# A triangular solve put on GpSimd, with halved and doubled tiles, fewer rows loaded and a new order

## The chip, the cores and the metric

The kernel runs on one core of a Trainium2 chip. The metric is the device time of one launch in microseconds (us), median of several runs. TensorE is called PE here, its weight loads PEld, VectorE is DVE, ScalarE is ACT, GpSimd is POOL, and SP is SyncE, the queue that issues every DMA of this kernel.

## The reference: a recurrent attention and two feed-forward layers

```python
def _attn_ref(r, k, v, w, a, b):            # each (4, 8, 768, 40)
    state = np.zeros((B, H, D, D))
    for t in range(S):
        y[:, :, t] = np.einsum('bhd,bhde->bhe', rt, state)
        Sa = np.einsum('bhde,bhe->bhd', state, at)
        state_decay = state * wt[:, :, None, :] - np.einsum('bhd,bhe->bhde', Sa, bt)
        state = state_decay + np.einsum('bhd,bhe->bhde', vt, kt)
    return y
...
    x = attn_out.transpose(0, 2, 1, 3).reshape(B * S, H * D)     # (3072, 320)
    h = x @ w_in;  g = h * (1.0 / (1.0 + np.exp(-h)));  x = g @ w_out     # layer 1, d_ff 2048
    h = x @ w_in2; g = np.maximum(0.01 * h, h);         out = g @ w_out2  # layer 2, d_ff 2048
```

The feed-forward weights arrive as float64; the kernel takes their words apart into floats ("decode").

## The kernel before, in words

**Attention in chunks.** The 768 steps are cut into 12 chunks of 64 steps. A chunk is two halves (two batches each), numbered x = 2c and x = 2c+1, so x runs from 0 to 23. Inside a chunk the recurrence is a triangular system per head, which is solved in two diagonal blocks of 32 by 32. Per x there are two functions, and per chunk a third:

- `pre(x)` (line 673) loads the decay products P and their reciprocals Q (tiles pt, qt), the rows of a, b and k, and builds on PE and DVE the triangular matrices (tiles sa, s2). The diagonal blocks go to DRAM (`s2d<-s`). The ring `sa` has four tiles, so `pre(x)` may start writing once the first products of `chain(x-4)` have read theirs; two GpSimd memsets (`sa<-`, 64x512) and a multiplication by P do that.
- `solve(c)` (line 724) loads both halves' blocks from DRAM, spread over the partitions, into `il_mm` ("ilm", one tile), and a start matrix into `il_y` ("ily", one tile) from a DRAM copy `il0d`. Then it does 31 elimination steps of two instructions each, a product into `il_t` ("ilt") and an addition into `il_y`, all `V.tensor_tensor`, thus DVE. The two alternate and each needs the one before. The inverse goes out in 8 DMAs (`yd<-ily`).
- `chain(x)` (line 748) loads the inverse (`yt<-yd`) and all other rows, and does the recurrent part: products of sa with the state (`bank<-tv,sa`), two products with the inverse (`bank<-carved,yt`), the state for x+2, and the output tile `xt`.

**Prefix products.** `prefix(g)` (line 624) makes the cumulative products of w for chunks 4g to 4g+3 in the tile `scratch`, and writes them, plain and transposed, to DRAM (`pd`, `ptd`), then their reciprocals (`qd`, `qtd`). Transposing is `transposed` (line 644): an ACT copy of 8 columns into a spare piece ("room") of `scratch`, then one DMA; 5 of these per matrix. For g = 1, 2 there is one room, so each copy waits for the DMA of the one before. `scratch` also serves the decoding of both layers' weights, in turn.

**Layers.** `moe_block` (line 489) does 256 tokens: transposes of two `xt` tiles, 16 pieces of the hidden dimension (products `bank<-xs,ih`, `il`, `i`; an activation on ACT; a remainder on DVE, `gs<-bank,gs`), and products `bank<-oh,gs`, `ol,gs`. Layer 1's block c needs chunk c's two x. Blocks of layer 1 fill PE between the steps of the attention. Layer 2 begins when the attention's tiles are released, and has 12 blocks of its own.

**What sets the order.** No operation is issued where it is written: `plan.record` (line 161) makes a task of it, and `Plan.run` (line 242) simulates the engines with estimated costs and issues, engine by engine, the task that can start first, and among several the one with the earliest due time. The due times come from the table `DUE` (line 339): per kind of work an offset for the first indices, one for the others, and a spread. `VG` tasks may go to DVE or POOL (`choose`, line 356). The order on each engine is thus fixed before the launch, and every engine works through its own list in order: an instruction that waits holds back all that stand behind it. All instructions recorded this way carry the line of `emit`, L370, so the trace is read by tile names.

Of the kernel before, what the change touches and what calls it, by code (L numbers as in the profile page):

```python
# [12 lines left out]
F32 = mybir.dt.float32  # L13
# [4 lines left out]
ALU = mybir.AluOpType  # L18
# [5 lines left out]
C = 64  # L24
# [34 lines left out]
class Plan:  # L59
# [172 lines left out]
    def hop(self, u, i, t, raw):  # L232
        e = u.engs[i]
        if e == "sync":
            return self.QUEUE + u.lat + self.LAND
        if t.engs == u.engs and not raw:
            return 0.0
        if e == "vector" and t.engs != u.engs:
            return 175.0
        return self.HOP[e]  # L240

    def run(self):
# [97 lines left out]
        "first": ((), -100.0, 0.0),  # L340
        "w1": ((-5.92, -26.13), 35.21, 2.15),
        "load": ((-1.55, -13.17, -4.18, -4.78, -3.25), -0.16, 1.0),
        "pre": ((-4.66, -13.38, -8.98, -1.31, -7.1), -7.87, 6.76),
        "solve": ((-3.08, -4.86, -4.85, -5.45, -11.98), -5.53, 4.21),
        "v": ((), 0.55, 0),
        "rows": ((), 5.99, 0),
        "chain": ((-0.56, -3.13, -3.14, 0.42, -3.28), 0.71, 0),
        "moe": ((0.74, 0.86, -0.46), -0.49, 4.78),
        "prefix": ((26.47, -11.65, 22.35), 25.65, 14.34),
        "w2": ((), 9.32, 10.91),  # L350
        "w2load": ((), 0.0, 0.2),
# [81 lines left out]
def attention_moe_kernel(  # L433
# [11 lines left out]
    x2d = dram.tile([NC, 2, 128, DM], F32, name="x2d")  # L445
    il0d = dram.tile([128, 8, 32], F32, name="il0d")
    w2d = dram.tile([128, 3 * DFF + NF * DM], F32, name="w2d")
# [9 lines left out]
    xo = [const.tile([128, DM], F32, name="xo")] * 2  # L457
    xt = Ring(const.tile([128, DM], F32, name=f"xt{i}") for i in range(4))
    gs = [const.tile([128, 2, TB], F32R, name=f"gs{i}") for i in range(3)]
# [29 lines left out]
    def moe_block(W, layer, get_x, put, gs, xs, xo, turn):  # L489
# [6 lines left out]
        for i in range(2):  # L496
            x = get_x(i)
            ps = plan.bank("h" if layer == 1 else "t", [128, 3, 128], False)
            with plan.group():
                for kt in range(2):  # L500
                    T.transpose(ps[:, kt, :], x[:, kt * 128 : kt * 128 + 128], ident)
                T.transpose(ps[0:64, 2, :], x[:, 256:DM], ident)
            h, l = xs[:, at[i], 0], xs[:, at[i], 1]
            A.copy(h[:, 0:2, :], ps[:, 0:2, :])
            A.copy(h[0:64, 2, :], ps[0:64, 2, :])
            A.copy(h[64:128, 2, :], ps[0:64, 2, :])
            V.tensor_tensor(out=l[:, 0:2, :], in0=ps[:, 0:2, :], in1=h[:, 0:2, :], op=ALU.subtract)
            V.tensor_tensor(out=l[0:64, 2, :], in0=ps[0:64, 2, :], in1=h[0:64, 2, :], op=ALU.subtract)
# [42 lines left out]
    with ExitStack() as c1:  # L551
# [5 lines left out]
        def one(shape, name):  # L557
            return ap.tile(shape, F32, name=name)
# [20 lines left out]
        uvts = many(1, [128, 2, 4, 2, 64], "uvt")  # L579
        zts = Ring(carved[:, 1, 1280 + 320 * i : 1600 + 320 * i].rearrange("p (v e) -> p v e", v=8) for i in range(2))  # L580
        s2s = one([128, 4, 16, 32], "s2")
        s2m = Ring(s2s[0:32, i] for i in range(4))
        s2rs = Ring(s2s[64:128, i, 0:8] for i in range(4))
        yt = many(2, [128, 8, 32], "yt")
        il_mm = one([128, 2, 32, 32], "ilm")
        il_y = one([128, 2, 8, 32], "ily")
        il_t = one([128, 2 * 76], "ilt")
        mask = one([128, 64], "mask")
        scratch = one([128, (C + 1) * (E + 8)], "scratch")

# [24 lines left out]

        il_0 = il_y[:, 0]
        G.memset(il_0, 0.0)
        for base, fill in ((0, -1.0), (32, 0.0)):
            G.affine_select(
                out=il_0, in_=il_0, pattern=[[-128, 8], [32, 32]], compare_op=ALU.is_gt, fill=fill, base=base, channel_multiplier=-1  # L620
            )
        SY.dma_start(out=il0d, in_=il_0)

        def prefix(g):
# [14 lines left out]

            room = il_mm.rearrange("p x i t -> p (x i t)") if g == 0 else wt  # L640
            n = 8 * (C + 1)
            rooms = itertools.cycle([room[:, n * i : n * i + n] for i in range(room.shape[1] // n)])

            def transposed(dst, x):
                for q in range(5):
                    z, qs = next(rooms)[:, : 8 * x.shape[2]].rearrange("p (e t) -> p e t", e=8), slice(8 * q, 8 * q + 8)
                    A.copy(z, x[:, qs])
                    SY.dma_start(
                        out=dst[4 * g : 4 * g + 4, :, qs].rearrange("c x e t -> (c x) (e t)"), in_=z.rearrange("p e t -> p (e t)")
                    )  # L650
# [97 lines left out]
        def chain(x):  # L748
# [19 lines left out]
            SY.dma_start(out=uvt[:, :, :, 1].rearrange("p b u t -> p (b u) t"), in_=xvt[x])  # L768
# [124 lines left out]
        for t in uv:  # L893
            VG.memset(t[0:64], 0.0)
        for t in tp + tt + rbd + uus:
            VG.memset(t, 0.0)
# [265 lines left out]
```

## Time and profile before

| | us |
|---|---|
| median of 3 runs | 1388.38 (1386.92 to 1392.41) |
| profiled execution | 1384.11, of which span 1382.1 |
| PE busy, DVE busy, ACT busy, POOL busy | 1094.7, 904.8, 690.6, 128.6 |
| mean granted TensorE clock | 0.911 |

How to read it: the span goes from the first to the last instruction. Layer 2 alone runs in the last 28% of it, attention and layer 1 together in the rest. Since each engine works in order, an engine's idle time is put down to what its next instruction was waiting for. Idle time counts only where that engine sets the end.

### The profile page before, as it was taken

The page shows a single profiled execution, that of the slowest core. Times are in us where ns is not written, and L with a number is a line of the kernel's source. Part 1 is how long each engine was busy: PE and PEld are TensorE (multiplying, and loading weights), DVE is VectorE, ACT ScalarE, POOL GpSimd, SP SyncE. Part 2 cuts the span into 40 slices and gives each one's busy share as a digit, 9 for nine tenths or more (in the row PEclk, how much of TensorE's full clock was granted, in tenths as well). Part 3 has the DMA queues.
Part 4 walks back from the last instruction along what each step waited for, and adds up shares of the span by engine and source line. Part 5 has one row for each costly group of instructions (what it writes and reads, how often), then busy time and mean ns, then how long its engine had stood idle before and what let it go on. Part 6 is the DMA issues. An engine that isn't in the chain of part 4 may idle for free.

```text
span 1382.1 us, 31698 instructions
## 1 busy us (share of the span) xinstructions
PE 1094.7 (79%) x12370; PEld 1034.3 (75%) x12370; DVE 904.8 (65%) x2211; ACT 690.6 (50%) x1760; POOL 128.6 (9%) x153
## 2 busy tenths in 40 slices
PE   1052077778888697888897879799899999999997
PEld 0041067667777596787787879789899999999997
DVE  8988688494758684858686759584555544445543
ACT  5444373444536364445454536465654444444443
POOL 3430014010310100002010000000000000000000
PEclk9985569798989899899999899899999999999999
DMA  9874347665858487575766766564511010000000
GB/s 220 200 185 139 97 121 167 128 173 115 186 133 186 120 192 164 138 178 133 172 165 149 163 157 157 144 135 106 164 55 28 20 30 20 20 20 25 16 11 22
DMA packets 356838, 164.09 MB, mean 119 GB/s; under 512 B 304712, under 2 KB 323272, under 8 KB 356296
## 3 DMA queue, kind: packets, MB, share of 16 engines
q1 hardware_dynamic: 356680, 161.99, 48.8%
q8 instruction: 99, 1.62, 0.5%
q14 instruction: 59, 0.48, 0.1%
HBM read 126.09 MB, written 35.84 MB: 117 GB/s over the span
## 4 chain that ended last, share of the span: by engine, by line
PE 46%; DMA 22%; DVE 19%; SPq 5%; ACT 4%; issue 4%; POOL 0%; DVEq 0%; ACTq 0%
PE bank L370 46%; DMA ilm<-s2d 6%; DVE scratch L370 5%; SPq L370 5%; DMA yd<-ily 3%; DVE ilt L370 3%; DVE ily L370 2%; DMA yt<-yd 2%; DVE carved L370 2%; DMA kb<-in_xkb_dram 2%; DVE sa L370 2%; DMA scratch<-in_moe_w_in_dram 2%; DMA w2d<-scratch 1%; ACT s L370 1%; DVE gs L370 1%
## 5 line engine op out<-in xcount | busy, mean ns | idle before, releaser
L370 PE MATMUL bank<-oh,gs 128*128 128x320 f32 x1344 | 362.5, 322 | 4.2 <-ACT xo L370 2.8
L370 PE MATMUL bank<-xs,ih 128*128 128x256 f32 x1536 | 310.4, 294 | 45.6 <-DVE gs L370 41.9
L370 PEld LDWEIGHTS bank<-xs,ih 128*128 128x128 f32 x1536 | 252.3, 196 | 53.5 <-DVE gs L370 47.4
L370 PEld LDWEIGHTS bank<-oh,gs 128*128 128x128 f32 x1344 | 245.1, 194 | 6.9 <-ACT xo L370 3.1
L370 PE MATMUL bank<-xs,il 128*128 128x256 f32 x768 | 221.8, 289 | 0.0
L370 PE MATMUL bank<-ol,gs 128*128 128x320 f32 x672 | 211.7, 315 | 0.0
L370 DVE TENSOR_TENSOR ilt<-ily,ilm 128x120 f32<-128x120 f32 (+24 forms) x372 | 111.9, 301 | 92.8 <-DMA ilm<-s2d 39.9
L370 PE MATMUL bank<-xs,i 128*128 128x256 f32 x768 | 158.4, 289 | 0.0
L370 DVE TENSOR_TENSOR gt<-bank,gt 128x256 f32<-128x256 f32 x192 | 81.4, 425 | 108.6 <-ACT gt L370 108.6
L370 PEld LDWEIGHTS bank<-xs,il 128*128 128x128 f32 x768 | 151.6, 197 | 0.0
L370 ACT ACTIVATE bank<-bank 128x256 f32<-128x256 f32 x192 | 70.8, 369 | 138.3 <-PE bank L370 137.0
L370 PEld LDWEIGHTS bank<-ol,gs 128*128 128x128 f32 x672 | 131.2, 195 | 0.0
L370 ACT ACTIVATE gt<-bank 128x256 f32<-128x256 f32 x192 | 73.6, 384 | 114.2 <-PE bank L370 113.7
L370 DVE TENSOR_TENSOR gs<-bank,gs 128x256 fp32r<-128x256 f32 x192 | 80.1, 419 | 75.8 <-ACT gs L370 74.4
L370 PEld LDWEIGHTS bank<-xs,i 128*128 128x128 f32 x768 | 123.7, 198 | 0.0
L370 DVE TENSOR_TENSOR ily<-ily,ilt 128x120 f32<-128x120 f32 (+24 forms) x372 | 106.7, 287 | 7.2 <-DMA yt<-yd 0.3
L370 ACT COPY carved<-bank 32x320 f32<-32x320 f32 (+1 forms) x184 | 65.3, 355 | 56.5 <-PE bank L370 51.0
L370 DVE TENSOR_TENSOR gs<-gt,gs 128x256 fp32r<-128x256 f32 x144 | 60.9, 423 | 48.4 <-ACT gs L370 46.8
L370 PE MATMUL bank<-gs,onesr 128*1 128x256 f32 (+1 forms) x40 | 16.1, 419 | 96.1 <-ACT gs L370 96.1
L370 PE MATMUL bank<-sa,kbt 128*128 128x128 f32 x384 | 60.4, 307 | 34.4 <-DVE kbt L370 30.8
L370 PE MATMUL bank<-carved,yt 32*32 32x40 f32 x1536 | 43.7, 217 | 52.3 <-DMA yt<-yd 51.1
L370 ACT CAST gs<-gt 128x256 fp32r<-128x256 f32 x144 | 58.3, 405 | 50.6 <-DVE gt L370 50.3
(121 smaller groups left out, 1856.2 us busy)
## 6 DMA issues: line engine op xcount, KB each, us to landing
kr<-in_xkb_dram SPq DMA_DIRECT2D x48, 256.0 KB
ilm<-s2d SPq DMA_DIRECT2D x24, 512.0 KB
kb<-in_xkb_dram SPq DMA_DIRECT2D x24, 320.0 KB
rp<-qd SPq DMA_DIRECT2D x48, 160.0 KB
uvt<-in_xvt_dram SPq DMA_DIRECT2D x24, 256.0 KB
carved<-in_xr_dram SPq DMA_DIRECT2D x48, 128.0 KB
carved<-in_xr_dram SPq DMA_DIRECT2D x24, 256.0 KB
scratch<-in_moe_w_out_dram SPq DMA_DIRECT2D x8, 640.0 KB
```

The lines of the kernel that those rows point to most:

```text
L370: getattr(eng, name)(*[real(x) for x in args], **{k: real(x) for k, x in kw.items()})
```

## The change

- **Engine.** The 62 instructions of `solve` go from DVE to POOL.
- **Matrix in halves.** `il_mm` is laid out so that the rows of steps 0 to 15 and of steps 16 to 30 are apart, each loaded by DMAs of its own: four of half the size in place of two. `il_y` has two tiles, chunk about. The start matrix stays in SBUF (`il_0`) and is copied by ACT (two copies a chunk); the DMA from `il0d` goes.
- **Fewer rows.** Inputs padded to 64 rows per head pair are loaded as 2 x 40 rows (R, uvt), with the rest cleared once. RB is no longer loaded but copied from R by ACT, two copies per x.
- **Room.** `xt` has 3 tiles for 4, `zts` 1 for 2, `scratch` 2880 columns for 3120. The room for `transposed` is halved: 10 copies of 4 columns and 10 DMAs in place of 5 of 8.
- **Order.** The planner's gap between two dependent POOL tasks is 80 ns for 150; the transposes of a layer 1 block take their bank like others; and a new table of due times.

```diff
-        return self.HOP[e]
+        return (80.0 if e == "gpsimd" and t.engs == u.engs else self.HOP[e])
...
-        "solve": ((-3.08, -4.86, -4.85, -5.45, -11.98), -5.53, 4.21),
+        "solve": ((-3.56, -4.67, -4.89, -5.93, -12.46), -13.61, 4.21),
...
-    xt = Ring(const.tile([128, DM], F32, name=f"xt{i}") for i in range(4))
+    xt = Ring(const.tile([128, DM], F32, name=f"xt{i}") for i in range(3))
...
-            ps = plan.bank("h" if layer == 1 else "t", [128, 3, 128], False)
+            ps = plan.bank("h" if layer == 1 else "t", [128, 3, 128])
...
-        zts = Ring(carved[:, 1, 1280 + 320 * i : 1600 + 320 * i].rearrange("p (v e) -> p v e", v=8) for i in range(2))
+        zts = Ring([carved[:, 1, 1280:1600].rearrange("p (v e) -> p v e", v=8)])
...
-        il_mm = one([128, 2, 32, 32], "ilm")
-        il_y = one([128, 2, 8, 32], "ily")
+        il_mm = one([128, 2, 2, 16, 32], "ilm")
+        il_ys = many(2, [128, 2, 8, 32], "ily")
+        il_0 = carved[:, 1, 1600:1856].rearrange("p (j t) -> p j t", j=8)
...
-        scratch = one([128, (C + 1) * (E + 8)], "scratch")
+        scratch = one([128, 3 * 3 * DM], "scratch")
...
-            n = 8 * (C + 1)
+            n = 4 * (C + 1)
...
-                for q in range(5):
-                    z, qs = next(rooms)[:, : 8 * x.shape[2]].rearrange("p (e t) -> p e t", e=8), slice(8 * q, 8 * q + 8)
+                for q in range(10):
+                    z, qs = next(rooms)[:, : 4 * x.shape[2]].rearrange("p (e t) -> p e t", e=4), slice(4 * q, 4 * q + 4)
...
-            for p in range(2):
-                SY.dma_start(
-                    out=il_mm[:, p].rearrange("p i t -> p (i t)"),
-                    in_=s2d[2 * c + p].rearrange("b h f i t -> (b h f) (i t)").unsqueeze(0).broadcast_to([4, 32, 1024]),
-                )
-            SY.dma_start(out=il_y.rearrange("p x j t -> p x (j t)"), in_=il0d.rearrange("p j t -> p (j t)").unsqueeze(1).broadcast_to([128, 2, 256]))
+            il_y = il_ys.at(c)
+            for p in range(2 if c > 0 else 0):
+                A.copy(il_y[:, p], il_0)
+            for f in range(2):
+                for p in range(2):
+                    SY.dma_start(
+                        out=il_mm[:, f, p].rearrange("p i t -> p (i t)"),
+                        in_=s2d[2 * c + p].rearrange("b h f (g i) t -> g (b h f) (i t)", g=2)[f].unsqueeze(0).broadcast_to([4, 32, 512]),
+                    )
...
-                V.tensor_tensor(
+                G.tensor_tensor(
                     out=t, in0=il_y[:, :, :J, i : i + 1].broadcast_to([128, 2, J, n]),
-                    in1=il_mm[:, :, i : i + 1, i + 1 : 32].broadcast_to([128, 2, J, n]), op=ALU.mult,
+                    in1=il_mm[:, i // 16, :, i % 16 : i % 16 + 1, i + 1 : 32].broadcast_to([128, 2, J, n]), op=ALU.mult,
                 )
-                V.tensor_tensor(out=il_y[:, :, :J, i + 1 : 32], in0=il_y[:, :, :J, i + 1 : 32], in1=t, op=ALU.add)
+                G.tensor_tensor(out=il_y[:, :, :J, i + 1 : 32], in0=il_y[:, :, :J, i + 1 : 32], in1=t, op=ALU.add)
...
-            SY.dma_start(out=R, in_=xr[x])
-            for o in range(2):
-                SY.dma_start(out=RB[64 * o : 64 * o + 64, :, o, :], in_=xr[x, 64 * o : 64 * o + 64])
+            for q in heads:
+                SY.dma_start(out=R[q], in_=xr[x, q])
...
+            for o, q in enumerate(heads):
+                A.copy(RB[q, :, o, :], R[q])
```

**Where the solve stands.** The list of DVE before, in the middle of the solve of chunk 8. `ilt` and `ily` are the solve, `scratch` is weight decoding, `gs` and `xt` belong to layer and output.

```order
L370 TENSOR_TENSOR ilt<-ily,ilm 128x96
L370 TENSOR_TENSOR gs_82<-bank_89,gs_82 128x256
L370 TENSOR_TENSOR ily<-ily,ilt 128x2x2x24
L370 TENSOR_TENSOR sa_129<-bank_91,mask 64x4x64
L370 TENSOR_TENSOR ilt<-ily,ilm 128x138
L370 TENSOR_SCALAR scratch<-scratch 128x640
L370 TENSOR_TENSOR ily<-ily,ilt 128x2x3x23
L370 SCALAR_TENSOR_TENSOR scratch<-scratch 128x640
L370 TENSOR_TENSOR ilt<-ily,ilm 128x132
```

The list of POOL now, in the solve of the same chunk.

```order
L370 MEMSET sa_127 64x8x64
L370 TENSOR_TENSOR ilt<-ily_135,ilm 128x104
L370 TENSOR_TENSOR ily_135<-ily_135,ilt 128x2x2x26
L370 TENSOR_TENSOR ilt<-ily_135,ilm 128x100
L370 TENSOR_TENSOR ily_135<-ily_135,ilt 128x2x2x25
L370 TENSOR_TENSOR ilt<-ily_135,ilm 128x96
L370 TENSOR_TENSOR ily_135<-ily_135,ilt 128x2x2x24
```

Before, the solve's steps alternate with other work of DVE; now they stand one behind the other on POOL, with four memsets of `sa` tiles among the 62, and DVE's list has none of them.

**Where the matrix is loaded.** The list of SP before, around the end of the solve of chunk 8.

```order
L370 DMA yd<-ily 256x1x32 x4
L370 DMA ilm<-s2d 128x1x1024
L370 DMA yd<-ily 256x1x32
L370 DMA ilm<-s2d 128x1x1024
L370 DMA yd<-ily 256x1x32 x3
L370 DMA kr_120<-in_xkb_dram 128x512
L370 DMA rp_111<-qd 64x640 x2
L370 DMA yt_134<-yd 128x8x32
L370 DMA ily<-il0d 128x2x256
L370 DMA yt_135<-yd 128x8x32
```

The list of SP now, around the same place.

```order
L370 DMA yd<-ily_135 256x1x32 x5
L370 DMA ilm<-s2d 128x1x512
L370 DMA yd<-ily_135 256x1x32 x3
L370 DMA tv_123<-in_xvo_dram 64x320 x2
L370 DMA kr_118<-in_xkb_dram 128x512
L370 DMA scratch<-in_moe_w_in_dram 128x1024
L370 DMA yt_132<-yd 128x8x32
L370 DMA s2d<-s_131 64x8x32
L370 DMA w2d<-scratch 128x512
L370 DMA yt_133<-yd 128x8x32
L370 DMA sa_125<-in_xa_dram 40x8x64 x2
L370 DMA ilm<-s2d 128x1x512 x2
```

The next matrix is now asked for in pieces: one load of steps 0 to 15 stands 12 rows above this piece, the other within the outgoing inverse, and both loads of the later steps behind the second `yt`. The load of the start matrix between the two `yt` is gone.

**Where chunk 4 enters.** The list of PE before, at the first product of x = 8 with its inverse (tile yt) and behind it: products of layer 1 (`xs`, `oh`, `ol`) all around.

```order
L370 MATMUL bank_89<-xs_109,i_103 128x256 x2
L370 MATMUL bank_93<-carved,yt_134 32x40 x16
L370 MATMUL bank_86<-oh_104,gs_81 128x320
L370 MATMUL bank_86<-ol_105,gs_81 128x320
L370 MATMUL bank_86<-oh_104,gs_81 128x320
```

The list of PE now, from the last layer product in front of x = 8's remaining steps; 43 rows with no layer product follow, of which the first five stand here.

```order
L370 MATMUL bank_85<-oh_102,gs_78 128x320
L370 MATMUL bank_88<-uv_121,kb_116 40x40 x16
L370 MATMUL bank_91<-ident,carved 128x128 x4
L370 MATMUL bank_90<-carved,yt_133 32x40 x16
L370 MATMUL bank_91<-carved,uvt_130 128x128 x4
L370 MATMUL bank_88<-carved,uvt_130 128x128 x4
```

Before, 3.6 blocks of layer 1 stand ahead of x = 8, and the rest of block 3 fills in around it; now all four blocks that can be done without chunk 4 are through, and the rest of x = 8, and x = 9, run with no layer product beside them. From chunk 6 on, a whole block stands ready beside each chunk in the new order.

## Rows read from the trace of the kernel before

**Rows 1.** Busy time in stretches from one even x's first yt product to the next's.
```profile
core 0: us, PE busy (x) PEld busy (x) DVE busy (x) ACT busy (x) POOL busy (x), PEclk, DMA share, GB/s
178.10:257.00 78.90, 58.23 (x720) 52.06 (x720) 57.76 (x139) 40.30 (x102) 22.47 (x27) 0.78 0.62 139
...
483.30:541.50 58.20, 53.02 (x732) 49.09 (x732) 41.46 (x116) 34.85 (x86) 4.12 (x4) 0.93 0.80 184
...
892.70:945.80 53.10, 49.23 (x794) 45.63 (x794) 36.62 (x108) 29.08 (x75) 2.10 (x1) 0.95 0.59 131
sum 767.70, PE 633.73 PEld 589.99 DVE 542.10 ACT 393.38 POOL 86.71; mean PE 57.61 PEld 53.64 DVE 49.28 ACT 35.76 POOL 7.88
```

**Rows 2.** Chain that ended last: its final pieces (start us, us, what).
```profile
983.51 390.11 PE bank L370 x2964
```

**Rows 3.** Waits of PE and POOL: us in total, times, longest.
```profile
POOL kb L370 <- DMA kb<-in_xkb_dram: 265.0, 9, 56.2
POOL sa L370 <- PE bank L370: 194.0, 7, 46.2
...
POOL sa L370 <- DMA sa<-in_xa_dram: 51.2, 4, 29.5
...
PE bank L370 <- DMA yt<-yd: 51.1, 10, 10.9
...
PE bank L370 <- DVE gs L370: 44.3, 23, 8.9
...
PE bank L370 <- DVE sa L370: 11.6, 4, 6.1
```

**Rows 4.** The page's groups of the solve on DVE.
```profile
L370 DVE TENSOR_TENSOR ilt<-ily,ilm 128x120 f32<-128x120 f32 (+24 forms) x372 | 111.9, 301 | 92.8 <-DMA ilm<-s2d 39.9
...
L370 DVE TENSOR_TENSOR ily<-ily,ilt 128x120 f32<-128x120 f32 (+24 forms) x372 | 106.7, 287 | 7.2 <-DMA yt<-yd 0.3
```

**Rows 5.** Timeline of DVE: solve of chunk 8 begins, ends; chunk 9's begins.
```profile
696.14 0.22 DVE L370 TENSOR_TENSOR ilt<-ily,ilm 128x62 f32<-128x62 f32 x1 [6.34 <-DMA ilm<-s2d]
...
741.16 0.19 DVE L370 TENSOR_TENSOR ily<-ily,ilt 128x16 f32<-128x16 f32 x1
...
765.17 0.22 DVE L370 TENSOR_TENSOR ilt<-ily,ilm 128x62 f32<-128x62 f32 x1 [11.72 <-DMA ily<-il0d]
```

**Rows 6.** Chain that ended last, in the stretch 680 to 770.
```profile
686.00 10.05 DMA ilm<-s2d
...
747.63 13.82 DMA yd<-ily
761.51 2.46 DMA yt<-yd
```

**Rows 7.** POOL's groups by form: count, busy, mean ns of one.
```profile
L370 POOL TENSOR_TENSOR scratch<-scratch 128x320 f32<-128x320 f32 x28 | 25.6, 916 | 12.3 <-DMA scratch<-in_w_dram 5.2 <-DMA uv<-in_xv_dram 5.1
...
L370 POOL MEMSET sa<- 64x512 f32 x40 | 21.6, 540 | 195.2 <-PE bank L370 194.0
...
L370 POOL TENSOR_TENSOR scratch<-scratch 128x640 f32<-128x640 f32 x2 | 3.1, 1568 | 14.1 <-issue 8.4 <-DVE scratch L370 5.7
```

**Rows 8.** Timeline of POOL: nine dependent products and their time together.
```profile
220.93 8.92 POOL L370 TENSOR_TENSOR scratch<-scratch 128x320 f32<-128x320 f32 x9 [5.21 <-DMA scratch<-in_w_dram]
```

**Rows 9.** Timeline, 719 to 724: a solve step alone, and one beside POOL.
```profile
719.25 0.28 DVE L370 TENSOR_TENSOR ilt<-ily,ilm 128x140 f32<-128x140 f32 x1
...
721.00 2.45 POOL L370 TENSOR_TENSOR sa<-sa,pt 40x512 f32<-40x512 f32 x2 [10.26 <-DMA sa<-in_xa_dram]
...
721.15 1.21 DVE L370 TENSOR_TENSOR ily<-ily,ilt 128x140 f32<-128x140 f32 x1
```

**Rows 10.** Timeline of ACT: prefix copies into the one room.
```profile
269.06 1.22 ACT L370 COPY scratch<-scratch 128x520 f32<-128x520 f32 x1
...
273.58 1.21 ACT L370 COPY scratch<-scratch 128x520 f32<-128x520 f32 x1
...
280.65 1.21 ACT L370 COPY scratch<-scratch 128x520 f32<-128x520 f32 x1 [0.32 <-DMA ptd<-scratch]
```

More of the change, by code (lines that the diff above doesn't have):

```diff
@@ L340 @@
         "first": ((), -100.0, 0.0),
-        "w1": ((-5.92, -26.13), 35.21, 2.15),
-        "load": ((-1.55, -13.17, -4.18, -4.78, -3.25), -0.16, 1.0),
-        "pre": ((-4.66, -13.38, -8.98, -1.31, -7.1), -7.87, 6.76),
-        "solve": ((-3.08, -4.86, -4.85, -5.45, -11.98), -5.53, 4.21),
[L345 to L350, printed above, removed]
+        "w1": ((-8.4, -23.65), 36.91, 2.03),
+        "load": ((-3.07, -14.35, -6.52, -6.22, -4.43), -1.98, 2.03),
+        "pre": ((-6.91, -15.06, -11.45, -1.23, -9.35), -10.11, 6.63),
+        "solve": ((-3.56, -4.67, -4.89, -5.93, -12.46), -13.61, 4.21),
+        "v": ((), -1.31, 0),
+        "rows": ((), 0.85, 0),
+        "chain": ((-0.19, -2.2, -2.86, 0.46, -3.64), -1.49, 0.05),
+        "moe": ((0.74, 0.32, -14.78), -0.59, 4.78),
+        "prefix": ((17.19, -20.66, 22.32), 16.09, 13.34),
+        "w2": ((), 10.7, 10.97),
         "w2load": ((), 0.0, 0.2),
@@ L445, in attention_moe_kernel @@
     x2d = dram.tile([NC, 2, 128, DM], F32, name="x2d")
-    il0d = dram.tile([128, 8, 32], F32, name="il0d")
     w2d = dram.tile([128, 3 * DFF + NF * DM], F32, name="w2d")
@@ L614, in attention_moe_kernel @@
             )
-        il_0 = il_y[:, 0]
-        G.memset(il_0, 0.0)
+        il_00 = il_ys[0][:, 0]
+        G.memset(il_00, 0.0)
         for base, fill in ((0, -1.0), (32, 0.0)):
             G.affine_select(
-                out=il_0, in_=il_0, pattern=[[-128, 8], [32, 32]], compare_op=ALU.is_gt, fill=fill, base=base, channel_multiplier=-1
+                out=il_00, in_=il_00, pattern=[[-128, 8], [32, 32]], compare_op=ALU.is_gt, fill=fill, base=base, channel_multiplier=-1
             )
-        SY.dma_start(out=il0d, in_=il_0)
+        A.copy(il_ys[0][:, 1], il_00)
+        A.copy(il_ys[1][:, 0], il_00)
         def prefix(g):
@@ L638, in prefix @@
             V.tensor_scalar(wp, wp, P_MIN / 2, P_MAX * 2, op0=ALU.max, op1=ALU.min)
-            room = il_mm.rearrange("p x i t -> p (x i t)") if g == 0 else wt
-            n = 8 * (C + 1)
+            room = il_mm.rearrange("p f x i t -> p (f x i t)") if g == 0 else wt
+            n = 4 * (C + 1)
             rooms = itertools.cycle([room[:, n * i : n * i + n] for i in range(room.shape[1] // n)])
             def transposed(dst, x):
-                for q in range(5):
-                    z, qs = next(rooms)[:, : 8 * x.shape[2]].rearrange("p (e t) -> p e t", e=8), slice(8 * q, 8 * q + 8)
+                for q in range(10):
+                    z, qs = next(rooms)[:, : 4 * x.shape[2]].rearrange("p (e t) -> p e t", e=4), slice(4 * q, 4 * q + 4)
                     A.copy(z, x[:, qs])
@@ L763, in chain @@
             VG.tensor_tensor(out=K, in0=K, in1=RP.rearrange("p b h e -> p (b h) e"), op=ALU.mult)
-            SY.dma_start(out=R, in_=xr[x])
-            for o in range(2):
-                SY.dma_start(out=RB[64 * o : 64 * o + 64, :, o, :], in_=xr[x, 64 * o : 64 * o + 64])
+            for q in heads:
+                SY.dma_start(out=R[q], in_=xr[x, q])
             UU, uvt = uus.at(x), uvts.at(x)
-            SY.dma_start(out=uvt[:, :, :, 1].rearrange("p b u t -> p (b u) t"), in_=xvt[x])
+            for q in heads:
+                SY.dma_start(out=uvt[q, :, :, 1].rearrange("p b u t -> p (b u) t"), in_=xvt[x, q])
             for b2 in range(2):
@@ L894, in attention_moe_kernel @@
             VG.memset(t[0:64], 0.0)
-        for t in tp + tt + rbd + uus:
+        A.copy(il_0, il_ys[1][:, 0])
+        for t in tp + tt + rbd + uus + rr + uvts:
             VG.memset(t, 0.0)
```

## The prediction

> **What bounds the kernel now.** I read the chain that ended last first, then PE's and DVE's load chunk by chunk, then PE's waits, and last the timeline and the chain through one chunk. At the end PE is full: from 983.5 us on the chain is nothing but PE, 390.1 us in 2964 products [rows 2]. A layer 2 block has 230 of them (16 pieces of 8 + 6 products, and 6 transposes), so this is 12.9 blocks of 30.3 us, and nothing in the change touches them. What can move is the part before. From the first product with an inverse (178.1 us) to that of the last chunk (945.8 us) there are 11 chunks in 767.7 us: 69.8 us each, of which PE is busy 57.6 [rows 1]. So PE is idle 12.2 us per chunk, 134 us in all. That it could go closer shows in single chunks: 58.2 us for the chunk from 483.3 us, 53.1 us for the last, against 78.9 us for the first [rows 1].
>
> The loop that sets the 69.8 us is the solve. In chunk 8 its first step begins at 696.14 us, its last at 741.16 us, and chunk 9's first at 765.17 us: a period of 69.0 us, of which 45.2 us are the solve and 23.8 us the turn-round [rows 5]. All 744 instructions take 111.9 + 106.7 = 218.6 us on DVE, 18.2 us a chunk [rows 4]; they are stretched to 45 us because DVE's own list puts other work between them. In the turn-round DVE sits idle 11.72 us for the start matrix, which may only be loaded when the outgoing inverse (13.82 us) has left the single tile; the matrix itself needs 10.05 us [rows 5, 6]. With one `ilm` and one `ily` none of this overlaps with the next solve. The result is late at PE: 51.1 us of PE's idle time end with the landing of `yt` [rows 3].
>
> **The change, part by part.**
>
> *The solve on POOL.* POOL's two-input products take 916 ns for 320 elements and 1568 ns for 640 [rows 7]: a slope of 2.04 ns per element and 264 ns fixed. The 62 instructions of a solve have 2 x 3120 elements (2·J·(31−i), summed over the 31 steps): 62 x 0.264 + 6240 x 0.00204 = 16.4 + 12.7 = 29.1 us. Nine dependent products took 8.92 us together, 0.99 us each, some 0.07 us above the mean of one [rows 7, 8]; 62 x 0.07 adds 4.5 us. Four memsets of 0.54 us stand among them [rows 7]. That gives 36 us. The trace shows no POOL product under 256 elements and none with broadcast operands, so the bounds: from below DVE's own 18.2 us, from above every one at the 320-element price, 62 x 0.986 + 2.2 = 63 us. I take 36, since the fit comes from the same instruction. Even 63 us is below the period of now.
>
> The Trainium skill, "GPSIMD Engine Reference", Engine selection, speaks against this part: elementwise work with two inputs belongs on VectorE, GpSimd being about half as fast. By that rule the solve would take 2 x 18.2 = 36.4 us (an estimate), which is what the rows give; slower as instructions, and still shorter than the 45.2 us that it lasts now.
>
> *Two result tiles, halved matrix, no `il0d`.* The next solve waits neither for the outgoing inverse nor for the start matrix, and its first half is loaded while this one's second half runs. Of the 23.8 us turn-round I expect less than 10 to remain, hidden since the solve now has 57.6 − 36 = 21 us to spare per chunk. The price: one SP issue more per chunk, and two ACT copies of 256 columns. With the two RB copies of 512 columns per x, at the 1.2 us that a copy of 520 takes [rows 10], ACT gets 4 x 1.2 + 2 x 0.6 = 6 us per chunk, beside 35.8 us of 69.8 [rows 1]; covered. If the cover went, it would be 11 x 6 = 66 us.
>
> *What PE gets back.* With the solve early, the 51.1 us for `yt` shrink to some 6: −45 us. DVE loses 18.2 of 49.3 us per chunk [rows 1, 4], 37%, so layer remainders (`gs`) stand behind fewer instructions; PE's 44.3 us for them and 11.6 us for `sa` [rows 3] fall by half, somewhat more than DVE's 37% since what stands last in a queue gains most: −28 us. PE's clock was 0.78 in the first chunk, which cost it 58.2 us busy, and 0.95 in the last [rows 1]; with fewer holes early: −5 us. Bounds for the three together: nothing, and the whole 134 us with the 5.
>
> *Fewer rows.* The loads shrink, RB's go. They lie beside other work with the DMA engines at 0.59 to 0.80 [rows 1]: nothing, or a few us of shorter flights, which I leave out.
>
> *Less room.* Three `xt` for four and one `zts` for two bind the attention closer to the layers; I take nothing. The prefix copies: cycles of copy and DMA take 4.5 and 7.1 us [rows 10]. Ten for five, for two matrices, is 10 cycles more per prefix: 45 to 71 us later, twice. Smaller DMAs shorten a cycle little. The cover is that attention is wanted only when the layers have caught up; the new PE list shows where it fails: at chunk 4, the first that needs prefix 1, four blocks are through and x = 8 and 9 run alone. A chunk of attention has 57.6 − 30.3 = 27.3 us of PE work, and the fastest chunk with a block took 53.1 us [rows 1, 2]; so PE loses at most 53.1 − 27.3 = 26 us there and at least nothing. I take 13: +13 us. That prefix 1 is later still is a risk for the range.
>
> *Start and planner.* Up to 100 us the work is the same; two memsets more. The gap constant and the due times act through the order alone.
>
> **The sum.** −45 − 28 − 5 + 13 = −65 us. The profiled execution took 1384.1 us (span 1382.1), 4.3 us less than the median of 1388.4; 1384.1 − 65 = 1319, on the scale of the median 1323 us. What is left idle in the 11 chunks is then 134 − 45 − 28 + 13 = 74 us, 6.7 per chunk, a period of about 64 us.
>
> **The rivals.**
>
> *Another loop takes over.* The way of a chunk from `pre` through s2d, ilm, solve, yd, yt stays in series, SP's list is in order, and POOL and DVE collide. Rows for the last: a solve step of 140 elements takes 0.28 us alone; the one that starts at 721.15, behind a POOL product with SBUF inputs, lasts 1.21 us, to 722.36, and POOL's first of two products ends at about 722.2 [rows 9]. So it stood until POOL let go. A chunk has some 18 DVE instructions with SBUF operands alone (two decodings, sa, kb); each can lose half a POOL product, 0.25 us, and POOL as much as their length, some 11 us: solve 47 us, DVE still below PE. With all that in series the period would be about 67: 11 x 2.8 = 31 us gained, 1357. For it: `yt` lands 23 us after the last step now [rows 5, 6], and that stays. Against: two chunks' time is there for it.
> The Trainium skill, "SBUF — State Buffer", Who interferes with whom, says that a DVE instruction with two SBUF inputs and a GpSimd one that reads SBUF exclude each other for their whole length; the trace agrees (1.21 against 0.28 us).
>
> *PE never waits.* All 134 us and the clock go: 1388 − 134 − 5, about 1250. For it: 53.1 us in one chunk. Against: that chunk has less work (49.2 us busy), and chunk 4 has its hole.
>
> *POOL's own list holds the solve up: slower.* Today POOL waits 194.0 us in 7 waits (27.7 each) for PE before a memset of `sa`, and 51.2 us in 4 (12.8 each) for the rows of a [rows 3]; nobody stands behind it. Now the rest of a solve does. One of each per chunk makes 36 + 40.5 = 76.5 us, over 69.8, and 11 x 6.7 = 74 us lost: 1462. It decides from 34 us of waits per solve on. Against: the memsets are placed where `chain(x-4)` should long have read, and the idle POOL of now reaches them too early, which makes the waits long.
>
> *No change.* What PE gains is lost at prefix 1 and 2 (71 us each at worst): 1388.
>
> **How the numbers follow.** My forecast has 0.60, its own range 1290 to 1350. The other loop 0.18 (1357), PE never waits 0.09 (1250), no change 0.05, slower 0.08. The range for 8 in 10 takes the first two whole and half of the third: 1255 to 1372. Faster by over 0.5% (about what a measurement of this kernel can tell from no change): 0.60 + 0.18 + 0.09 = 0.87; within it 0.05; slower 0.08.
>
> **What would show it.** Right: solves of 33 to 45 us on POOL that start within 10 us of the one before when the matrix is there; chunks of 60 to 66 us at unchanged PE work; PE's wait for `yt` under 15 us, for `gs` under 30; a hole of PE at x = 8 and 9. Wrong: POOL instructions of 100 elements that take over 0.7 us; long POOL waits inside a solve; PE's waits for `yt` unchanged, or a new wait for `qt` or `pt` before chunk 4 or 8 of more than 30 us.

## The result: 1372.5 us, and the profile after

The changed kernel takes 1372.54 us (1371.26 to 1377.18) against 1390.39 for the kernel before in the same runs: a ratio of 0.9878, 95% interval 0.9841 to 0.9914, some 18 us faster. Forecast were 1323 us and a range up to 1372, so the time lies half a microsecond outside it; the gain is a little over a quarter of the 65 us that were expected.

The page's line of busy times, of the kernel after. The same 12370 PE instructions ran as before.

```profile
PE 1100.0 (80%) x12370; PEld 1041.4 (76%) x12370; DVE 759.1 (55%) x1498; ACT 728.1 (53%) x1863; POOL 408.7 (30%) x868
```

The span went from 1382.1 to 1371.1 us while PE's busy time rose from 1094.7 to 1100.0. So PE's time without work (span less busy) fell from 287.4 to 271.1 us: 16 us, of which PE's longer busy time took 5 back. These 5 are the clock's: the trace's clock records are at full speed (2.4 GHz) or half (1.2 GHz), and in the stretches at half speed PE was busy 142.5 us, before 132.1. Half of that difference is 5.2 us. All runs below are judged by idle and busy time.

The stretches of the kernel after, from one even x's first yt product to the next's, with columns as in [rows 1]:

```profile
180.80:241.30 60.50, 44.85 (x662) 40.80 (x661) 30.84 (x67) 36.49 (x93) 24.83 (x47) 0.87 0.62 136
...
354.70:486.10 131.40, 106.69 (x1126) 100.67 (x1126) 51.30 (x100) 62.30 (x160) 55.96 (x121) 0.87 0.54 127
486.10:524.40 38.30, 28.54 (x591) 24.97 (x591) 28.86 (x37) 23.05 (x60) 9.68 (x26) 0.90 0.53 119
524.40:603.60 79.20, 66.14 (x820) 62.14 (x820) 31.60 (x61) 40.99 (x104) 28.75 (x68) 0.85 0.65 144
...
860.50:912.20 51.70, 50.52 (x769) 47.54 (x771) 29.58 (x57) 34.65 (x86) 28.45 (x62) 1.00 0.54 130
sum 731.40, PE 619.92 PEld 578.39 DVE 382.72 ACT 414.09 POOL 325.62; mean PE 56.36 PEld 52.58 DVE 34.79 ACT 37.64 POOL 29.60
```

The sum is 36.3 us shorter than in [rows 1], yet PE's time without work in it only went from 134.0 to 111.5 us. The rest of the 36 us is layer work that now comes later: the last chunk begins 33.6 us earlier, but from there to the end it takes 458.9 us for 436.3. A shorter stretch is no gain by itself. Two things stand out. The first four chunks took 305.3 us (180.8 to 486.1), before 305.2 (178.1 to 483.3): nothing won. The last seven took 60.9 us each, before 66.1. And the hole is there: 131.40 us up to the first yt product of x = 8.

PE's waits over the whole run, answering to [rows 3] (us in total, times, longest):

```profile
PE bank L370 <- DVE gs L370: 36.2, 17, 8.0
PE bank L370 <- DMA yt<-yd: 16.5, 7, 4.0
PE bank L370 <- ACT carved L370: 14.6, 17, 4.2
PE bank L370 <- DVE sa L370: 6.9, 3, 3.8
```

`yt` fell by 34.6 us of 51.1, `sa` by 4.7 of 11.6, but `gs` only by 8.1 of 44.3. ACT's copies into `carved`, behind which PE had waited 2.5 us, stand at 14.6.

The solve, as the page's group and in POOL's timeline of chunks 8 and 9, answering to [rows 4, 5]:

```profile
L370 POOL TENSOR_TENSOR ilt<-ily,ilm 128x120 f32<-128x120 f32 (+24 forms) x372 | 158.9, 427 | 238.6 <-DMA ilm<-s2d 186.1
```

```profile
676.25 0.29 POOL L370 TENSOR_TENSOR ilt<-ily,ilm 128x62 f32<-128x62 f32 x1 [36.04 <-DMA ilm<-s2d]
...
712.31 0.23 POOL L370 TENSOR_TENSOR ily<-ily,ilt 128x16 f32<-128x16 f32 x1
...
739.62 0.76 POOL L370 TENSOR_TENSOR ilt<-ily,ilm 128x62 f32<-128x62 f32 x1 [18.23 <-ACT carved L370]
...
773.62 0.45 POOL L370 TENSOR_TENSOR ily<-ily,ilt 128x16 f32<-128x16 f32 x1
```

36.3 and 34.5 us from first step to last. Between these two solves 27.1 us pass, more than the 23.8 of before. Over the run POOL stands idle between solves mostly for the next matrix (186.1 us in all). But the chain that ended last no longer goes through the solve here, as it did in [rows 6]: between 665 and 740 us it is 85% PE's own work, with this as its longest piece.

```profile
681.16 45.11 PE bank L370 x595
```

Last, the chain that ended last, in the hole (start us, us, what):

```profile
456.42 3.08 PE bank L370 x22
...
459.70 7.14 DMA ptd<-scratch
466.86 0.02 ACT scratch L370
...
467.46 0.37 ACT gs L370
...
467.86 0.44 DVE gs L370
...
468.34 1.86 PE bank L370 x7
```

This is how the small room reaches PE: ACT's next copy of prefix 2 waits 7.14 us for the DMA that empties the room; the layer's `gs` copy stands behind it in ACT's list; DVE's remainder waits for that, and PE for the remainder. The row of PE's waits names DVE, which had nothing to do with it. Going back from each of PE's `gs` waits to what DVE and ACT were doing gives the same picture: before, 28.0 of 43.7 us had DVE's own list behind them and 15.8 ACT's; now it is 7.7 and 28.1 of 35.8 us.

### The profile page after: what moved, and what is told of

Read it like the earlier page. It is cut to its first block, busy times and chain, and to the rows that moved or that the text cites. A ratio compares the mean times of both kernels' runs of the same rounds, so it can differ in the third digit from the quotient of the medians.

```text
span 1371.1 us, 31938 instructions
## 1 busy us (share of the span) xinstructions
PE 1100.0 (80%) x12370; PEld 1041.4 (76%) x12370; DVE 759.1 (55%) x1498; ACT 728.1 (53%) x1863; POOL 408.7 (30%) x868
## 4 chain that ended last, share of the span: by engine, by line
PE 47%; DMA 19%; POOL 9%; ACT 8%; DVE 6%; issue 5%; SPq 5%; ACTq 0%; POOLq 0%; DVEq 0%
PE bank L370 47%; SPq L370 5%; POOL ily L370 3%; POOL ilt L370 3%; DVE scratch L370 3%; DMA carved<-in_xr_dram 3%; ACT carved L370 2%; DMA ilm<-s2d 2%; POOL scratch L370 2%; DMA ptd<-scratch 2%; DMA w2d<-scratch 2%; DMA scratch<-in_moe_w_out_dram 1%; DMA kr<-in_xkb_dram 1%; DMA yd<-ily 1%; DMA qt<-qtd 1%
## 5 line engine op out<-in xcount | busy, mean ns | idle before, releaser
L370 POOL TENSOR_TENSOR ilt<-ily,ilm 128x120 f32<-128x120 f32 (+24 forms) x372 | 158.9, 427 | 238.6 <-DMA ilm<-s2d 186.1
L370 POOL TENSOR_TENSOR ily<-ily,ilt 128x120 f32<-128x120 f32 (+24 forms) x372 | 160.8, 432 | 28.0
L370 PE MATMUL bank<-sa,kbt 128*128 128x128 f32 x384 | 64.3, 321 | 50.7 <-DVE kbt L370 44.6
L370 PEld LDWEIGHTS bank<-sa,kbt 128*128 128x128 f32 x384 | 57.2, 228 | 55.3 <-POOL kb L370 25.8
L370 PEld LDWEIGHTS bank<-gs,onesr 128*1 128x1 f32 x40 | 3.4, 86 | 109.2 <-ACT gs L370 108.9
L370 ACT CAST gs<-gt 128x256 fp32r<-128x256 f32 x144 | 58.2, 405 | 49.8 <-DVE gt L370 49.5
```

Source lines behind the costliest of these rows:

```text
L370: getattr(eng, name)(*[real(x) for x in args], **{k: real(x) for k, x in kw.items()})
```

## The experiments

"Full room" is the kernel after with the prefix room of before (5 copies of 8 columns). Ratios are to the kernel before on the same chip; 0.01 is 14 us. "PE idle" is span less busy of the profiled execution. That is one execution, and it can lie off the median of its runs (after_pv 8 us below, solve_dve 6 above), so small differences of the last three columns say little.

| run | ratio (95%) | span | PE busy | PE idle |
|---|---|---|---|---|
| after | 0.9878 (0.9841 to 0.9914) | 1371.1 | 1100.0 | 271.1 |
| null | 0.9880 (0.9858 to 0.9901) | 1368.2 | 1095.3 | 272.9 |
| room8 | 0.9616 (0.9590 to 0.9641) | 1335.2 | 1085.3 | 249.9 |
| solve_dve | 1.0021 (0.9994 to 1.0047) | 1392.5 | 1115.6 | 276.9 |
| solve_dve_room8 | 0.9811 (0.9769 to 0.9853) | 1370.7 | 1100.5 | 270.2 |
| before_pool | 1.0188 (1.0143 to 1.0233) | 1421.1 | 1108.8 | 312.3 |
| rb_dma | 1.0135 (1.0106 to 1.0165) | 1402.4 | 1109.5 | 292.9 |
| rb_room8 | 0.9896 (0.9850 to 0.9942) | 1382.4 | 1110.9 | 271.5 |
| rb_none_room8 | 0.9622 (0.9589 to 0.9654) | 1337.8 | 1086.0 | 251.8 |
| after_pv | 0.9783 (0.9753 to 0.9812) | 1351.9 | 1098.8 | 253.1 |
| room8_pv | 0.9735 (0.9699 to 0.9772) | 1358.9 | 1102.7 | 256.2 |
| room8_land | 0.9613 (0.9566 to 0.9660) | 1340.8 | 1096.0 | 244.8 |
| old_due_room8 | 0.9655 (0.9625 to 0.9684) | 1337.9 | 1096.9 | 241.0 |
| room8_split | 0.9781 (0.9747 to 0.9815) | 1359.5 | 1103.1 | 256.4 |
| room8_whole | 0.9575 (0.9547 to 0.9603) | 1334.9 | 1097.4 | 237.5 |
| room8_merge | 1.0863 (1.0824 to 1.0903) | 1519.1 | 1136.4 | 382.7 |
| rb_merge_room8 | 1.0862 (1.0818 to 1.0907) | 1508.2 | 1127.4 | 380.8 |
| whole_dvecopy | 0.9680 (0.9647 to 0.9712) | 1349.0 | 1094.4 | 254.6 |
| room8_nosolve | 0.9768 (0.9735 to 0.9800) | 1361.1 | 1112.8 | 248.3 |

**The room** (room8, and the scatter of the order, null).

```diff
-        scratch = one([128, 3 * 3 * DM], "scratch")
+        scratch = one([128, (C + 1) * (E + 8)], "scratch")
-            n = 4 * (C + 1)
+            n = 8 * (C + 1)
```

and 5 copies of 8 columns for 10 of 4, hence 30 ACT copies and 30 DMAs fewer in all; `ilt` and `pc` move into free columns of `carved` to make place. null has `"solve": ((-3.50, ...` for `((-3.56, ...`.

> The prefix copies have their full room again, 5 copies of 8 columns per matrix (il_t and pc moved into free columns of carved to make place). Theory B: the last q of prefix 1 leaves near 350 us in place of 385, the chunk period of 131 us at chunk 4 falls to about 105, and PE's idle 24.7 us there falls under 8; time about 1352 us. Theory A: only ACT's waits for ptd and qtd (41.8 us) fall to about 24, PE gets back about 5 us, 1367; the hole stays above 15 us.

> One due time changed by 0.06 of its unit and nothing else: what the order alone scatters. Both theories: 1372 us within 5. If it moves by more, differences of that size between the other runs are not to be read as causes.

Null stayed within 2 us. room8 gained 36 us, more than theory B asked. Its stretches, columns as above:

```profile
368.90:456.90 88.00, 69.15 (x890) 64.33 (x889) 51.92 (x79) 44.59 (x111) 31.96 (x73) 0.90 0.49 120
...
sum 703.40, PE 604.59 PEld 564.79 DVE 388.06 ACT 411.74 POOL 331.87; mean PE 54.96 PEld 51.34 DVE 35.28 ACT 37.43 POOL 30.17
```

The last q of prefix 1 left at 346 us for 385, and chunk 4 began at 456.9 us for 486.1; the seven chunks from there took the same (425.4 and 426.1 us). But PE's idle time in the 131 us of the hole was 24.7 us and in the 88.0 us is still 18.9 (in the kernel before 19.9): the idle part of theory B fell. What the room cost is 21 us of PE idle, of which 6 in the hole and 18 behind it (with 2 less ahead of it), and 15 us of PE busy time, at a mean clock of 0.915 for 0.929. Whether the waits for the room or the 30 issues more bring this, the pair does not tell.

PE's waits in room8, whole run:

```profile
PE bank L370 <- DVE gs L370: 21.6, 16, 5.5
PE bank L370 <- ACT uv L370: 17.8, 16, 5.7
PE bank L370 <- ACT carved L370: 17.1, 20, 3.3
...
PE bank L370 <- DMA yt<-yd: 7.5, 4, 2.7
...
PE bank L370 <- DVE sa L370: 1.3, 2, 1.1
```

The kinds of wait that the forecast spoke of are nearly gone, and two of ACT's are new.

**The engine** (solve_dve, solve_dve_room8, before_pool).

```diff
-                G.tensor_tensor(
+                V.tensor_tensor(
-                G.tensor_tensor(out=il_y[:, :, :J, i + 1 : 32], ...
+                V.tensor_tensor(out=il_y[:, :, :J, i + 1 : 32], ...
```

before_pool is the reverse edit in the kernel before, with the planner's gap and the transposes' bank of the changed kernel.

> The changed kernel with the 62 instructions of a solve on DVE again; halves, two results, rows, room and due times stay. If the engine is what gave the gain: PE's waits for gs behind DVE's queue come back (28 us in place of 7.7) and yt gets late: about 1395 us (1385 to 1405). If the double tiles and the order gave it: 1366 to 1378.

> room8 with the solve on DVE again: what the engine is worth where the prefix does not set the time. With the small room the engine was worth 18 us (1389 against 1371). If the forecast's terms hold (yt and gs wait for DVE): 1336 + 40 = 1376 (1365 to 1390). If the two results and the split matrix did most of it: 1340 to 1352.

> The kernel before with the solve on GpSimd (gap constant 80, and the bank of the layer 1 transposes taken as in the changed kernel, without which the planner finds no order); one ilm, one ily, start matrix by DMA, full prefix room, old due times. The forecast's turn-round argument: 36 us solve and 23.8 us turn-round are a period of 60 us, still no longer than PE's work, so yt's 51 us shrink by half: about 1355 us. Rival (the single tiles keep the loop, or due times made for DVE place POOL's list badly): 1380 to 1400.

GpSimd is worth 20 us with the small room (1.0021 - 0.9878; some 23 were expected) and 27 with the full one (0.9811 - 0.9616; 40 were expected). Both times fell where "the engine gave it" had put them, but `yt` did not get late: with the solve on DVE again PE waits for it 10.6 us (small room) and 9.6 us (full room), for 51.1 in the kernel before. The 11 chunks of solve_dve_room8:

```profile
PE bank L370 <- DVE gs L370: 48.3, 22, 9.3
...
PE bank L370 <- DMA yt<-yd: 9.6, 6, 2.6
```

So the fall of `yt` is not the engine's. It is not the due table's (old_due_room8, 9.6 us) nor the RB copies' (rb_room8, 13.8) either, and with R and uvt loaded whole it is still 19.6 (room8_whole). No run has the two result tiles or the halved matrix alone. What the engine gives PE is `gs`: 48.3 us against 20.5 in room8, and with the small room 28.6 us behind DVE's own list against 7.7. In span, the engine is worth 20 us of PE's idle time with the full room and 6 with the small one, and 15 us of its busy time in each.

By itself, with single tiles, the engine costs 26 us. A first and a last step of solve in before_pool, chunks 8 and 9, and its wait for yt:

```profile
720.42 0.29 POOL L370 TENSOR_TENSOR ilt<-ily,ilm 128x62 f32<-128x62 f32 x1 [34.50 <-DMA yt<-yd]
...
756.35 0.23 POOL L370 TENSOR_TENSOR ily<-ily,ilt 128x16 f32<-128x16 f32 x1
...
789.34 0.29 POOL L370 TENSOR_TENSOR ilt<-ily,ilm 128x62 f32<-128x62 f32 x1 [32.76 <-DMA qt<-qtd]
```

```profile
PE bank L370 <- DMA yt<-yd: 75.4, 9, 15.5
```

The solve takes the 36 us it should, but the turn-round is 32.8 us (before 23.8, [rows 5]), so the period stays 69 us. In that company the engine does not pay; in the company of the change's other edits, the two result tiles among them, it does. Which of them it needs is not shown.

**RB** (rb_dma, rb_room8, rb_none_room8).

```diff
-            for o, q in enumerate(heads):
-                A.copy(RB[q, :, o, :], R[q])
+            for o, q in enumerate(heads):
+                SY.dma_start(out=RB[q, :, o, :], in_=xr[x, q])
```

(behind the loads of R; rb_none_room8 has neither.)

> The two ACT copies that fill RB from R go; RB is loaded by DMA again (2 x 40 rows). Theory A (ACT's in-order list: copies that wait for a DMA hold up the layers behind them): in the changed kernel ACT waits 30.8 us in 16 waits for the rows of r, and about 17 us of PE's idle time end behind them; so these go, time about 1358 us (1352 to 1365). Theory B (the halved prefix room and the hole at chunk 4 ate the gain): no change, 1368 to 1377.

> room8 (1336 us) with RB loaded by DMA in place of ACT's two copies per x. Theory A (ACT's list stands at copies that wait for the rows of r; by the trace of room8 some 16 to 18 us of PE's idle time end behind them): about 1322 us (1314 to 1330), and the waits of ACT for the rows of r (26.5 us) gone. The loss of 34 us that the same edit brought with the small room is then the prefix's (its last q of prefix 2 left 30 us later). Rival (the extra DMAs in SP's list cost more than ACT's waits): 1345 us or more, with PE's waits for kbt above 20 us.

> room8 without RB: neither loaded nor copied, the products read the zeros set at the start. What the two copies per x cost in all. Theory A (copies that wait for a DMA hold ACT's list): PE's 16 to 18 us behind them go, 1318 to 1324 us. Rival (the forecast's 'covered'): 1332 to 1340. A time above 1345 would say that the order that the planner finds for another set of tasks weighs more than either.

Theory A fell in its simple form, and RB's loads made both kernels slower where it had forecast faster. Leaving the copies out moves nothing (0.9622 for 0.9616), though PE's waits behind them in room8, walked back through the engines' lists, add up to some 12 to 16 us: other waits took their place. Loading RB instead costs 36 us with the small room and 39 with the full one, and not by the wait that the rival named: in rb_room8 PE waits under 6 us for `kbt` in the chunks.

**Prefix earlier, other order** (after_pv, room8_pv, old_due_room8, room8_land).

```diff
-            PV = V if g == 0 else G
+            PV = V
```

room8_land has `QUEUE, LAND = 800.0, 3350.0` for `800.0, 1350.0`; old_due_room8 has the table `DUE` of before.

> The changed kernel (half room) with the 14 products of prefix 1 and 2 on DVE in place of GpSimd, where those of prefix 1 stood behind solve 1 until 242 us. If the lateness of prefix 1 makes the hole at chunk 4: its last q leaves some 15 us earlier (near 370 in place of 385), the period of 131 us falls to about 115, time about 1355 us (1348 to 1362). If the hole comes from the copies' hold on ACT's and SP's lists, wherever they lie: 1368 to 1377.

> The same with the full room. There prefix 1 leaves at 346 us and its chunk takes 88 us in place of some 62, so by the lateness theory 15 us earlier is still worth about 10: 1326 us (1318 to 1332), the fastest of all so far. If the room alone decides: 1333 to 1340. If the products are in the way of DVE's remainders (gs): 1342 or more.

> room8 with the due times of the kernel before. If the edits themselves make the gain: within 10 us of room8, 1330 to 1346. If the table does much of it: 1355 to 1390, with the solves late again (PE's waits for yt above 25 us).

> room8 with one planner constant changed: a DMA is taken to land 3.35 us after its bytes in place of 1.35, so that what waits for it is put later in the lists. Theory A (the lists of ACT and DVE hold instructions that wait for a DMA and hold up what stands behind them): ACT's waits for DMAs (some 88 us in 43 waits in room8) fall by half, PE's idle behind them from about 45 us to 20, time about 1312 us. Rival (these waits are the chain's own latency): later starts make the chain longer, 1340 to 1360.

after_pv gained 13 us, but not in the way expected: prefix 1 left at 370 us, yet chunk 4 began at 483.5, hardly earlier; the gain is in the last seven chunks (415.7 us for 426.1) and behind them. In room8 the same edit loses 17 us. In the four pairs (after, solve_dve, rb_dma and after_pv against their full-room twins) the full room brings chunk 4 forward by 29, 14, 30 and 27 us and the end by 36, 29, 33 and 7 us (the 7 lie inside the intervals). The table is worth 5 us, hence little. With later landings in the plan ACT's `uv` and `carved` waits fell from 34.0 to 12.1 us, as theory A had it, and the time stayed: other waits came again (chunk 4 began at 478 us).

**SP's list** (room8_split, room8_whole, room8_merge, rb_merge_room8).

```diff
 room8_split
-                SY.dma_start(out=KR, in_=xkb[x, :, hb])
+                for h4 in range(2):
+                    SY.dma_start(out=KR[:, 4 * h4 : 4 * h4 + 4], in_=xkb[x, :, 8 * b2 + 4 * h4 : 8 * b2 + 4 * h4 + 4])
 room8_whole
-            for q in heads:
-                SY.dma_start(out=R[q], in_=xr[x, q])
+            SY.dma_start(out=R, in_=xr[x])
 room8_merge
+                in_=qd[c, :, hs].rearrange("t x e -> t (x e)").unsqueeze(0).broadcast_to([2, 64, 640]),
+                in_=pd[c, :, hs].rearrange("t (b h) e -> b t (h e)", b=2),
```

room8_whole loads uvt whole in the same way; of room8_merge the new sources of `rp` and `pa` stand here.

> room8 with kr loaded in two DMAs in place of one: 48 issues more, same bytes. Theory S: some 35 us more as with RB's loads, 1360 to 1385. Rival: 1330 to 1345.

> room8 with R and uvt loaded whole as in the kernel before (128 rows, zeros among them), one DMA each in place of two: 48 issues less, 6 MB more. What 'fewer rows' is worth. Theory S: issues weigh more than bytes, so a gain, 1315 to 1330. Rival (bytes, or flights, bind): 1345 to 1360; the forecast's own 'nothing or a few us': 1333 to 1342.

> room8 with pa and rp loaded by one DMA each per x in place of two: 48 issues less in SP's list, same bytes. Theory S (SP's list, 0.7 us per issue and 484 us of issuing in 705 us, holds up what stands behind): SP gets back some 30 us, time 1305 to 1325. Rival (order of the plan, or nothing waits for SP): 1330 to 1345.

> RB by DMA, not by copies (48 issues more), and pa and rp merged (48 less): as many issues as room8. Theory S: room8's time within 8 us, 1328 to 1345, in place of rb_room8's 1383. Rival (RB's bytes, its 256-byte pieces, or the place of its loads): 1365 to 1385.

48 issues more cost 23 us; 48 fewer, with 5 MB more (154.5 for 149.8), gave 6, so the narrower loads of R and uvt show no gain. The merged loads cost 173 us, for a reason of their own (last section), and with RB loaded beside them the ratio is 1.0862: neither says anything on the issues. Theory S is half borne out and not settled.

**What is left** (whole_dvecopy, room8_nosolve).

```diff
-                    A.copy(z, x[:, qs])
+                    (A.copy if g == 0 else V.tensor_copy)(z, x[:, qs])
...
-            for i in range(31):
+            for i in (0, 30):
```

> room8_whole (0.9575 of before) with the prefix copies of prefix 1 and 2 on DVE in place of ACT. If ACT's list is what holds the layers up: PE's 13 us behind these copies go, ratio 0.945 to 0.952 (about 1320 us), the fastest of all. If the head of a list that waits for a DMA costs as much on DVE, or another wait follows at once: 0.955 to 0.965.

> room8 with 2 of the 31 elimination steps (the other 29 are left out). If the solve is hidden behind PE, as forecast: 0.955 to 0.965 of before, as room8 (0.962). If its 36 us still are on the loop of a chunk: 0.935 to 0.95, PE's idle time in the 11 chunks under 75 us in place of 98.

Without the copies ACT's list is freer and the time 15 us longer. Without most of the solve neither range was met (0.9768). PE is idle 248.3 us, with the solve 249.9, and the time is 21 us longer because PE's busy time is:

```profile
PE 1112.8 (82%) x12370; PEld 1053.4 (77%) x12370; DVE 734.8 (54%) x1480; ACT 721.7 (53%) x1833; POOL 127.1 (9%) x190
```

This is the clock: PE was busy 168.7 us in the stretches at half speed, in room8 110.1. The sign that the expectation named failed too: from the first inverse to the last the 11 chunks take 770.7 us with 134.5 of them idle (703.4 and 98.8 in room8), but they begin 47 us earlier. So PE's idle time over the whole run does not hang on the solve's length, as far as a run with another order can show it. room8 and room8_whole beat both kernels, the one before by 3.8 and 4.3%.

## Why the prediction was wrong, point by point

*The solve on POOL: right in length, in part by luck.* 36 us (33 to 45) were forecast; chunks 2 to 11 took 31 to 42 us, 35 on average (the first two 44 and 67, with waits between steps). But the fit overprices short steps: a step of 100 elements takes 0.36 us at its shortest where the fit says 0.47, and the 62 steps at their shortest add up to 23.0 us for the fit's 29.1. Beside DVE they get longer, to 26.6 us on average, and this the forecast had left to a rival. 58 of the 744 steps took over 0.7 us, 16 of them among the 168 of 96 to 108 elements, which had been named a sign against the fit. The same step beside a DVE product with SBUF inputs, and alone:

```profile
685.30 0.98 POOL L370 TENSOR_TENSOR ily<-ily,ilt 128x132 f32<-128x132 f32 x1
685.30 1.53 DVE L370 TENSOR_TENSOR sa<-sa,pt 40x512 f32<-40x512 f32 x2
...
700.81 0.45 POOL L370 TENSOR_TENSOR ily<-ily,ilt 128x132 f32<-128x132 f32 x1
```

All 81 steps that were over 0.2 us longer than the shortest of their form had a decoding, an `sa` or a `kb` instruction of DVE beside them; of the 517 that had none, not one was. So the first rival's collision is real, at 3.6 us a solve where it put 11. The rival that POOL's own list makes it slower did not come: POOL's waits for PE before `sa` fell from 194.0 to 38.6 us.

*Two tiles, turn-round hidden: half right.* The period from chunk 4 on is 60.9 us (60 to 66 forecast; 66.5 over all 11 chunks, and 63.9 in room8). The turn-round did not shrink to under 10 us: it is 27.1, since the matrix comes later. It is hidden all the same, as the chain through chunk 8 shows. With single tiles the period stayed at 69 (before_pool), in a kernel without the other edits as well.

*"What PE gets back", -45 - 28 - 5: the step that failed first.* In room8, where prefix 1 is as early as before, the named waits fell as forecast: yt by 43.6 us, gs by 22.7 and sa by 10.3 (against [rows 3]), 77 us where 73 were put. But PE's idle time fell by 37.5. The step added up waits as if each were time won. When they went, PE stopped next at copies of ACT (uv and carved: 34.0 us in the 11 chunks, before 8.2), and when those were taken away (room8_land, rb_none_room8, whole_dvecopy) at others. Nine of the thirteen runs with the full room lie at 237 to 256 us of idle time, the one without most of the solve among them. The step should have asked what is late next. Its clock term, 5 us, came to 9 in room8 and was lost in the changed kernel.

*"Less room", +13: mis-sized by two to three times in three pairs of four.* Prefix 1 is late, 34 us after that of before (45 to 71 forecast), and the hole is where it was put: 24.7 us idle, inside the bound of 26. But room8 idles 18.9 us in the same place, so the hole itself cost some 6 us and the step's 13 were not lost there. The cost was 36 us between after and room8 (29, 33 and 7 in the other pairs). The step counted PE's loss in the hole alone; it left out that chunk 4 and all behind it begin 29 us later with the layers used up, that ACT's list stands still at the room, and that PE runs the same work at a lower clock (142.5 us busy at half speed, 110.1 in room8). The fewer `xt` and `zts`, put at nothing, have no run.

*Edits costed at nothing.* The ACT copies of RB: right, covered. The due times: right, 5 us. "Fewer rows, nothing or a few us": wrong for RB, whose loads cost 36 to 39 us when they come back; so the copies that replace them won about what the room lost.

The sum: 23 us of the miss are the room (36 for 13), 25 the waits (78 us forecast without the room, 53 measured as 0.9616); together 48 of the 49.5 by which 1323 was missed. This is bookkeeping with one pair: the 53 hold what RB won, which the forecast did not count, so the terms that it named brought less. The first rival (another loop takes over, 1357) and "no change" (1388) both lie 15.5 us off. The first was not right by its loop of solve, yd and yt; the second, that the gain is lost at the prefix, is nearer to what the runs show.

*Open.* Why idle time settles at 237 to 256 us; why RB's loads cost 36 us; which of the edits beside the engine took `yt` away; and why three edits that take work off an engine cost 15 to 21 us. For two of the three the trace names the term, not its cause: PE is busy longer at half speed (168.7 us in room8_nosolve and 153.0 in room8_pv, 110.1 in room8); in whole_dvecopy it is idle 17 us longer than in room8_whole. Each edit gives another order on all engines. null and old_due_room8 moved 0 and 5 us, so this scatter is not there for every edit, but differences under some 20 us between single full-room runs are not read as causes here; the room, the engine and RB rest on pairs.

## What to carry to other kernels

Waits of the busiest engine do not add up to a gain: remove one and the next late input stops it, so bound the sum by a run, or at least an estimate, in which the suspect is left out. When an in-order list holds an instruction that waits for a DMA, charge it with all that stands behind, on every engine down the line; a wait row names only the last link. When a buffer for staging is halved, ask what starts later for it, not only what idles.

## What was not expected of the hardware

Loading `rp` and `pa` by one DMA each in place of two made things worse by 173 us (1.0863 against 0.9616). In the packet records one merged load of `rp` (128 packets of 2560 bytes, 0.10 to 0.12 us each) lasts 6.4 to 7.7 us from first start to last end, about two packets at a time; in room8 the 64 packets of one half load are through in 0.8 to 1.0 us at some 0.15 us each, about ten at a time. Loads that were not merged come late as well. DVE's waits for the load of `kb` between 180 and 1000 us, in room8 and then in room8_merge:

```profile
DVE kb L370 <- DMA kb<-in_xkb_dram: 14.4, 4, 5.9
```

```profile
DVE kb L370 <- DMA kb<-in_xkb_dram: 49.6, 17, 7.2
```

The merged source has a leading dimension of 2. The Trainium skill, "DMA: Bandwidth & Descriptors", Rules for kernel authors, states that an outermost dimension of fewer than 16 entries confines a DMA to at most that many engines; two at a time agrees. The same table advises one 128-partition transfer in place of two halves; here that was the costliest edit of all, with the merged source written with the halves outermost. How the 173 us come together from the late loads was not followed further.

And PE's clock moves the result beside its waits: the same 12370 instructions are 1085.3 us busy at a mean granted clock of 0.929 (room8), 1100.0 at 0.915 (after) and 1136.4 at 0.867 (room8_merge). What counts is how long PE works at half speed: 110.1, 142.5 and 225.9 us. Busy time less half of that is 1030.3, 1028.7 and 1023.5 us (1028.7 in the kernel before), so all of the 15 us of busy time between room8 and after are the clock's. The mean over the span hides this, since it also counts stretches at half speed in which PE idles: 0.911 before and 0.915 after, though PE's busy time rose.
